# Block-wise turning through DRAM for the last layer's first six tiles, and other gather chunks

## Chip, cores and metric

One core of one Trainium2 chip. The metric is the device time of one execution in microseconds (us), as the median of several runs. PE is TensorE, DVE is VectorE, ACT is ScalarE, POOL is GpSimd and SP is SyncE, which here only issues DMAs.

## What is computed

The reference is an attention over 4 x 576 tokens with 8 heads of 64, then a mixture of 8 experts (top 2 of 8 per token, 512 to 1024 to 512), then one dense layer of 512 to 2048 to 512 with a leaky activation. The last two parts, cut to what matters here:

```python
def _moe_ref(x, w_gate, w_noise, noise, w1, w2):       # x: 2304 x 512
    ...                                                # top2, top2_w: two experts a token and their weights
    for e in range(E):
        for k in range(2):
            mask = top2[:, k] == e
            h = np.maximum(x[mask] @ w1[e], 0.0)
            out[mask] += top2_w[mask, k, None] * (h @ w2[e])

def _moe2_ref(x, w_in, w_out, alpha):
    h = x @ w_in                                       # 2304 x 2048
    g = np.maximum(h, 0.0) + alpha * np.minimum(h, 0.0)
    return g @ w_out
```

## The kernel before

The order of the work on every engine is written out by hand: instructions stand in an engine's queue in the order in which the program issues them, and each engine works its queue strictly in that order. Every product is done in three matmuls on a high and a low part of both operands (hi x hi, lo x hi, hi x lo), so each operand is split once: ACT copies the high part, DVE or POOL subtracts it for the low part.

**Tokens** go in 18 tiles of 128. Each expert has a block of two tiles and a block of three. The expert outputs are stored by slot into the DRAM tensor `yg` (L242). The last layer takes them back in token order. For one tile T it does these steps:

- `y_load(T)`: two indirect DMAs (L901), issued by POOL, gather the two expert rows of each token from `yg` into two row buffers (`m_rows`, `m_tmp`, and `m_v` for tile 0). Called gathers below.
- `combine(T)`: ACT scales the first row by its weight (L908), DVE adds the second row times its weight (L909).
- the turn: the last layer needs the tile with its 512 features on the partitions. There are two ways in the program. One is four PE transposes (L203) into a PSUM bank. The other stores the combined tile into the DRAM tensor `xs` (L1040), loads it back with four DMAs in 32x32 blocks that are already in their turned places (`blocked`, L186), and lets DVE turn the inside of every block in one instruction (L200).
- `x_split`: after the turn, ACT copies the high part out of PSUM (L206) and DVE subtracts it for the low part (L207).

**The last layer** runs over five groups of tiles, called j = 0 to 4: tiles 0 and 1, then four times four tiles. In each there are 16 chunks f of 128 hidden features. `up_chunk` is 12 matmuls (L214) into one of three PSUM banks of the ring `ps_t`; DVE applies the leaky part with two instructions (L995, L996) into a ring of four half buffers, ACT copies the high part (L999), POOL subtracts it for the low part (L1000). `down_chunk` of the same chunk follows two chunks later (L1019): per tile it reads the high, the low and the high part of the chunk in turn. `next_x(j, f)` puts the tile steps of group j + 1 between the chunks of group j. The turns of `x_split` take the bank `ps_v` for the first tile of a group and banks of the ring `ps_t` for the other three.

**Weights** of the last layer come from DRAM on SP's queue (L166, slots 72 to 79), two raw buffers deep. ACT copies the high part (L171), and POOL, or DVE for slots 72 to 74, subtracts the low part (L177). In group j = 0 the slots 75 to 79 are split at chunks 1, 3, 5, 7 and 9. The next load of a raw buffer waits for the low part of the slot before in that buffer.

**Before the change** tiles 0 and 1 are gathered during the last expert's second block, at its up chunks 5 and 7, combined during the first tile of its down products and turned by PE during the second tile. Tiles 2 to 5 are gathered at chunks 4, 6, 8 and 10 of j = 0, combined two chunks later and turned by PE two chunks after that. Tiles 6 to 17 already go through `xs` and DVE.

Of the kernel before, what the change touches and what calls it, by code (L numbers as in the profile page):

```python
# [33 lines left out]
def emit(tc, qt, kt, v, tau, wg, wn, noise, w1, w2, w_in, w_out, alpha, out):  # L34
# [3 lines left out]
    pe, dve, act, pool, sp = nc.tensor, nc.vector, nc.scalar, nc.gpsimd, nc.sync  # L38
# [4 lines left out]
    with (  # L43
# [9 lines left out]
        xs = dp.tile([N, DM], FT, name="xs")  # L53
# [126 lines left out]
        xrows = {}  # L180

        def blocked(dst, src):

            src = src.rearrange("(j a) (c i b) -> i a c j b", j=4, c=HP, i=4)
            for i in range(4):
                sp.dma_start(dst[i * 32:i * 32 + 32].rearrange("a (c j b) -> a c j b", c=HP, j=4), src[i])  # L186
# [10 lines left out]
        def x_split(src, j, x, bank=None, is_blocked=True):  # L197
            ps = (bank or (psum_v, psum_t, psum_t, psum_t)[j])()
            if is_blocked:
                dve.transpose(ps, src)  # L200
            else:
                for c in range(HP):
                    pe.transpose(ps[:, c * 128:c * 128 + 128], src[:, c * 128:c * 128 + 128], ident)  # L203
            pv_ = ps.rearrange("p (c t) -> p c t", c=HP)
            xh = x[0][:, :, j * 128:j * 128 + 128]
            act.copy(xh, pv_)  # L206
            dve.tensor_tensor(x[1][:, :, j * 128:j * 128 + 128], pv_, f32(xh), op=OP.subtract)  # L207
# [460 lines left out]
        for b in range(1, B):  # L668
            o = 20 * b
# [68 lines left out]
        for i in range(END):  # L738
# [27 lines left out]
            if outs:  # L766
                pv(iv)
                if units[iv][2] == HP - 1 or iv < SOLO:
                    T = group_evac(iv)
# [38 lines left out]
        X = (cut(m_x, 0, [HP, 384], FR), cut(m_x, 1536, [HP, 384], FR))  # L808
# [74 lines left out]
        for n in range(W0, 72):  # L883
            t = 1 + 3 * (n - W0)
# [11 lines left out]
        yrows = {}  # L896

        def y_load(T, src):
            for k in range(2):
                r = row_tile()  # L900
                pool.indirect_dma_start(  # L901
                    out=r, out_offset=None, in_=src,
                    in_offset=bass.IndirectOffsetOnAxis(ap=posi[:, T, k:k + 1], axis=0))
                yrows[T, k] = r

        def combine(T):
            y0, y1 = yrows[T, 0], yrows[T, 1]
            act.activation(y0, y0, AF.Copy, scale=wts[:, T, 0:1])  # L908
            dve.scalar_tensor_tensor(y1, y1, wts[:, T, 1:2], y0, op0=OP.mult, op1=OP.add)  # L909

        near = yg[0:N + E * BLOCK0]
        blocks = [(0, bt), (bt, CAP // 128)]
# [19 lines left out]
        for e in range(E):  # L932
            wc = [8 * e + d for d in range(4)]
            wc2 = [8 * e + 4 + d for d in range(4)]
            for bi, (t0, t1) in enumerate(blocks):
                if (e, bi) == (0, 0):
                    continue
                n = (t1 - t0) * 128
                nxt = (e, 1) if bi == 0 else (e + 1, 0)
                last = nxt[0] == E  # L940
                u0, u1 = blocks[nxt[1]]
                for f in range(8):
                    relu(f, n, mm1(psum_1(f), n, wc, X, f * 128), HS)
                    tick()
                    if last and f in (5, 7):
                        y_load((f - 5) // 2, near)
                left, owed = list(range(u1 - u0)), []
                for t in range(t1 - t0):
                    ps = psum_s()[:, 0]
                    for f in range(0, 8, 2):  # L950
                        mm2(ps, t, n, [f, f + 1], 8, wc2, HS)
                        if f % 4 == 0 and left and (t > 0 or not last):
                            j = left.pop(0)
                            x_split(yrows[j, 1] if last else xrows.pop((nxt[0], u0 + j)), j, X, None, not last)
                            if not last:
                                owed.append(j)
                        elif f % 4 == 2:
                            if last and t == 0:
                                combine(f // 4)
                            if owed:  # L960
                                owed.pop()
                                next_row()
                            tick()
                    y_store(e, t0 + t, ps)
# [62 lines left out]
        def next_x(j, f):  # L1027

            if j + 1 == len(sizes):
                return  # L1030
            T, x = sum(sizes[:j + 1]), XS[j + 1 if j < 1 else 2 - (j + 1) % 2]
            for t in range(4):
                o = 4 + 2 * t if j == 0 else 3 * t
                if f == o:
                    y_load(T + t, yg[:, :])
                if f == o + 2:
                    combine(T + t)
                    if j > 0:
                        back = xs[(T + t) * 128:(T + t) * 128 + 128]
                        sp.dma_start(back, yrows[T + t, 1])  # L1040
                        blocked(yrows[T + t, 0], back)
                if f == o + 4:
                    x_split(yrows.pop((T + t, 0 if j else 1)), t, x, None, j > 0)

        chunks = [(j, f) for j in range(len(sizes)) for f in range(16)]
        for i in range(len(chunks) + 2):
# [127 lines left out]
```

## Time and profile before

| what | value |
|---|---|
| median of 3 runs | 1166.37 us (1166.24 to 1168.17) |
| the profiled execution, its own time | 1170.81 us |
| its span in the trace | 1169.1 us |
| PE busy | 1135.2 us, 97% of the span |
| DVE, ACT, POOL busy | 53%, 46%, 46% |
| granted PE clock, mean | 0.997 of full speed |

The span is what the trace covers; the profiled execution's own time has 1.7 us around it. The profiled execution is 4.4 us above the median of the unprofiled runs. A row of the timeline gives the start in us from the span's start, the busy time, the engine, the line, the operation with what it writes and reads, and how many instructions are merged into it; in brackets stands how long the engine had been idle before it and what ended that.

### The profile page before, as it was taken

To read this page: it belongs to the slowest core of one execution; us is meant where nothing else is said; L and a number is where in the kernel's file an instruction comes from. 1 tells how busy PE (TensorE), PEld (TensorE's weight loads), DVE (VectorE), ACT (ScalarE), POOL (GpSimd) and SP (SyncE) were. 2 spreads that over 40 slices of the span, in tenths; PEclk is the share of its full clock that TensorE was granted. 3 is DMA by queue.
4 is the path that set the end of the run, shared out by engine and by line. 5 is a ranking of instruction groups with operands and counts; after the bars stand their busy time and mean duration, and the time that the engine had idled before them with its cause. 6 is when DMAs were issued, how large, how long until landed. Compare 5 with 4: busy or idle time off the path is not lost. (4 is left out here: it accounts for less than half of the span.)

```text
span 1169.1 us, 20453 instructions
## 1 busy us (share of the span) xinstructions
PE 1135.2 (97%) x7754; PEld 977.5 (84%) x7754; DVE 622.8 (53%) x1332; ACT 532.0 (46%) x1039; POOL 532.8 (46%) x632
## 2 busy tenths in 40 slices
PE   7999989999899999999999999999999999999997
PEld 6887777877789999999989898998888888888886
DVE  7978788899644544454545453445443343342221
ACT  7977768788624544444444454433211211211111
POOL 7636534654524545455454555556332333332221
PEclk9999999999999999999999999999999999999999
DMA  7423222132357676567667565541321321320001
GB/s 219 137 86 122 92 77 74 73 119 92 136 141 207 184 199 194 183 171 213 192 189 202 186 188 190 166 151 54 86 66 25 92 66 27 90 64 10 36 1 39
DMA packets 156552, 141.50 MB, mean 121 GB/s; under 512 B 108576, under 2 KB 109216, under 8 KB 156448
## 3 DMA queue, kind: packets, MB, share of 16 engines
q1 hardware_dynamic: 150400, 120.91, 35.1%
q0 software_dynamic: 5760, 18.88, 4.8%
q8 instruction: 63, 1.03, 0.4%
q14 instruction: 41, 0.34, 0.1%
q10 hardware_dynamic: 288, 0.34, 0.1%
HBM read 97.11 MB, written 42.99 MB: 120 GB/s over the span
## 5 line engine op out<-in xcount | busy, mean ns | idle before, releaser
L214 PE MATMUL ps_t<-m_v,m_pair 128*128 128x384 f32 (+2 forms) x1216 | 220.0, 317 | 0.3 <-DVE m_v L207 0.3
L177 POOL TENSOR_TENSOR m_pair<-m_v,m_pair 128x512 fp32r<-128x512 f32 x114 | 151.9, 1353 | 130.0 <-ACT m_pair L171 106.7
L214 PEld LDWEIGHTS ps_t<-m_v,m_pair 128*128 128x128 f32 x1216 | 186.8, 190 | 8.1 <-DVE m_v L207 0.5
L232 PE MATMUL ps_s<-m_pair,m_hh 128*128 128x512 f32 x528 | 167.5, 390 | 0.0
L995 DVE TENSOR_SCALAR m_tmp<-ps_t,alpha_t 128x512 f32<-128x512 f32 (+1 forms) x80 | 55.7, 697 | 208.6 <-PE ps_t L214 200.9
L225 DVE SCALAR_TENSOR_TENSOR m_gate<-ps_t,m_hh 128x384 fp32r<-128x384 f32 (+1 forms) x120 | 58.8, 493 | 169.9 <-ACT m_hh L224 169.8
L399 DVE SCALAR_TENSOR_TENSOR m_hh<-m_tmp,sm,m_hh 128x576 f32<-128x576 f32 x144 | 126.1, 908 | 2.4 <-ACT sm L380 2.0
L214 PE MATMUL ps_t<-m_v,m_early 128*128 128x256 f32 (+2 forms) x672 | 127.3, 320 | 0.0
L232 PEld LDWEIGHTS ps_s<-m_pair,m_hh 128*128 128x128 f32 x528 | 99.1, 188 | 20.3
L1000 POOL TENSOR_TENSOR m_v<-m_tmp,m_v 128x512 fp32r<-128x512 f32 x39 | 50.4, 1293 | 139.7 <-ACT m_v L999 139.7
L375 DVE TENSOR_SCALAR_CACHE_REDUCE m_tmp<-ps_s 128x576 f32<-128x576 f32 x144 | 103.6, 752 | 18.5 <-PE ps_s L364 16.0
L386 ACT ACTIVATE m_hh<-m_tmp,sm 128x576 f32<-128x576 f32 x144 | 105.7, 783 | 11.0 <-DVE m_tmp L375 10.9
L214 PEld LDWEIGHTS ps_t<-m_v,m_early 128*128 128x128 f32 x672 | 105.9, 189 | 5.1 <-DVE m_v L207 0.4
L364 PE MATMUL ps_s<-m_pair 64*128 64x288 f32 (+1 forms) x864 | 95.3, 318 | 12.9 <-DVE m_tmp L375 8.3
L999 ACT CAST m_v<-m_tmp 128x512 fp32r<-128x512 f32 x39 | 24.2, 620 | 173.5 <-DVE m_tmp L996 173.5
L232 PE MATMUL ps_s<-m_pair,m_gate 128*128 128x512 f32 x264 | 102.9, 390 | 0.0
L224 ACT ACTIVATE m_hh<-ps_t 128x384 fp32r<-128x384 f32 (+1 forms) x120 | 52.7, 439 | 98.3 <-PE ps_t L214 96.8
L1000 POOL TENSOR_TENSOR m_gate<-m_tmp,m_gate 128x512 fp32r<-128x512 f32 (+1 forms) x41 | 44.1, 1077 | 116.1 <-ACT m_gate L999 109.9
L364 PEld LDWEIGHTS ps_s<-m_pair 64*128 64x128 f32 (+1 forms) x864 | 72.3, 191 | 28.1 <-DVE m_tmp L375 14.3
L1019 PE MATMUL ps_s<-m_pair,m_v 128*128 128x512 f32 x396 | 95.1, 389 | 0.0
L1019 PE MATMUL ps_s<-m_pair,m_gate 128*128 128x512 f32 x360 | 88.3, 391 | 0.0
L1019 PEld LDWEIGHTS ps_s<-m_pair,m_v 128*128 128x128 f32 x396 | 74.3, 188 | 15.4
(229 smaller groups left out, 1982.0 us busy)
## 6 DMA issues: line engine op xcount, KB each, us to landing
m_v<-in_w_dram SPq DMA_DIRECT2D x64, 512.0 KB
yg<-m_tmp SPq DMA_DIRECT2D x40, 256.0 KB
m_tmp<-in_w_in_dram SPq DMA_DIRECT2D x16, 512.0 KB
m_tmp<-in_w_out_dram SPq DMA_DIRECT2D x16, 512.0 KB
m_early<-in_kt_dram SPq DMA_DIRECT2D x15, 320.0 KB
yg<-m_gate SPq DMA_DIRECT2D x18, 256.0 KB
m_rows<-xg SPq DMA_DIRECT2D x72, 64.0 KB
out_dram<-m_tmp SPq DMA_DIRECT2D x18, 256.0 KB
```

The lines of the kernel that those rows point to most:

```text
L177: eng.tensor_tensor(WL[n][:, w], raw[:, w], f32(WH[n][:, w]), op=OP.subtract)
L214: pe.matmul(ps[:, :n], w[wc[d]][:, col:col + 128], x[xx][:, d, :n], start=(k == 0), stop=(k == 11))
L224: act.activation(h, ps, AF.Relu)
L225: dve.scalar_tensor_tensor(hs[1][:, f * n:f * n + n], ps, 0.0, f32(h), op0=OP.max, op1=OP.subtract)
L232: pe.matmul(ps, a[:, o:o + 128], ww[w][:, c:c + 512], start=(f == 0 and k == 0), stop=(f == nf - 1 and k == 2))
L364: pe.matmul(u["ps", h][:, x, :288], lhs, kk[r, o:o + 288], start=(k == 0), stop=(k == 2))
L375: dve.tensor_scalar(u["sp"][:, h].rearrange("p (a b) -> p a b", a=2), ps[:, :, :288], -0.125, None, op0=OP.mult, op1=OP.min, accum_out=u[" ...
L386: act.activation(u["em"][:, h], u["sp"][:, h], AF.Exp, bias=u["sm"][:, h:h + 1], scale=-1.0)
L399: dve.scalar_tensor_tensor(u["em"][:, h], u["sp"][:, h], sm[:, 2 + h:3 + h], u["em"][:, h], op0=OP.is_le, op1=OP.mult, accum_out=acc)
L995: dve.tensor_scalar(g, ps, 0.0, alpha_t[:, f:f + 1], op0=OP.min, op1=OP.mult)
L1000: pool.tensor_tensor(h[:, n:2 * n], g, f32(h[:, :n]), op=OP.subtract)
L1019: pe.matmul(ps, h[x][:, t * 128:t * 128 + 128], ww[w][:, c:c + 512], start=(f == 0 and k == 0), stop=(f == 15 and k == 2))
```

## The change

Tiles 0 to 5 now take the second way, like tiles 6 to 17: `combine` itself stores every tile to `xs`, and a new function `reload` brings it back in blocks. `x_split` is called in its form for blocks everywhere, so no PE transpose is left in the last layer. In the last expert's second block, tiles 0 and 1 are gathered at up chunks 1 and 3, combined at 4 and 6 and reloaded at 6 and 7. In j = 0, tiles 2 to 5 are gathered at chunks 1, 3, 6 and 9, combined two chunks later, reloaded one chunk after that and turned five chunks after their gathers. In the later groups the gather, the combine and the turn stand where they stood.

```diff
             dve.scalar_tensor_tensor(y1, y1, wts[:, T, 1:2], y0, op0=OP.mult, op1=OP.add)
+            sp.dma_start(xs[T * 128:T * 128 + 128], y1)
+
+        def reload(T):
+            blocked(yrows[T, 0], xs[T * 128:T * 128 + 128])
...
-                    if last and f in (5, 7):
-                        y_load((f - 5) // 2, near)
+                    if last:
+                        if f in (1, 3):
+                            y_load(f // 2, near)
+                        if f in (4, 6):
+                            combine(f // 2 - 2)
+                        if f in (6, 7):
+                            reload(f - 6)
...
-                            x_split(yrows[j, 1] if last else xrows.pop((nxt[0], u0 + j)), j, X, None, not last)
+                            x_split(yrows.pop((j, 0)) if last else xrows.pop((nxt[0], u0 + j)), j, X)
...
-                            if last and t == 0:
-                                combine(f // 4)
...
-                o = 4 + 2 * t if j == 0 else 3 * t
+                o, wait = (3 * t, 4) if j else ((1, 3, 6, 9)[t], 5)
                 if f == o:
                     y_load(T + t, yg[:, :])
                 if f == o + 2:
                     combine(T + t)
-                    if j > 0:
-                        back = xs[(T + t) * 128:(T + t) * 128 + 128]
-                        sp.dma_start(back, yrows[T + t, 1])
-                        blocked(yrows[T + t, 0], back)
-                if f == o + 4:
-                    x_split(yrows.pop((T + t, 0 if j else 1)), t, x, None, j > 0)
+                if f == o + wait - 2:
+                    reload(T + t)
+                if f == o + wait:
+                    x_split(yrows.pop((T + t, 0)), t, x)
```

POOL's queue at the start of the last layer, before (L1000 is a chunk's low part, L177 a weight's low part in two halves, L901 a gather), from the low parts of chunks 0 and 1 on:

```order
L1000 TENSOR_TENSOR m_gate<-m_tmp,m_gate 128x256 x2
L177 TENSOR_TENSOR m_pair<-m_v_73,m_pair 128x512 x2
L1000 TENSOR_TENSOR m_gate<-m_tmp,m_gate 128x256 x2
L177 TENSOR_TENSOR m_pair<-m_v_73,m_pair 128x512 x2
L1000 TENSOR_TENSOR m_gate<-m_tmp,m_gate 128x256
L901 DMA m_rows<-yg,posi 128x512 x2
L1000 TENSOR_TENSOR m_gate<-m_tmp,m_gate 128x256
L177 TENSOR_TENSOR m_pair<-m_v_73,m_pair 128x512 x2
L1000 TENSOR_TENSOR m_gate<-m_tmp,m_gate 128x256
L901 DMA m_tmp<-yg,posi 128x512 x2
```

The same stretch of POOL's queue after the change (L1007 is the former L1000):

```order
L1007 TENSOR_TENSOR m_gate<-m_tmp,m_gate 128x256 x2
L177 TENSOR_TENSOR m_pair<-m_v_73,m_pair 128x512 x2
L901 DMA m_rows<-yg,posi 128x512 x2
L1007 TENSOR_TENSOR m_gate<-m_tmp,m_gate 128x256 x2
L177 TENSOR_TENSOR m_pair<-m_v_73,m_pair 128x512 x2
L901 DMA m_tmp<-yg,posi 128x512 x2
L1007 TENSOR_TENSOR m_gate<-m_tmp,m_gate 128x256 x2
L177 TENSOR_TENSOR m_pair<-m_v_73,m_pair 128x512 x2
L1007 TENSOR_TENSOR m_gate<-m_tmp,m_gate 128x256
L901 DMA m_rows<-yg,posi 128x512 x2
```

The gathers of tiles 2 and 3 now stand directly behind the low parts of weights 75 and 76 and ahead of the low parts of chunks 2 and 4.

DVE's queue in the same group after the change, from the combine of tile 2 (L909) to the turn of tile 3 (L1002 and L1003 are the former L995 and L996, chunks 4 to 8):

```order
L909 SCALAR_TENSOR_TENSOR m_rows<-m_rows,wts 128x512
L1002 TENSOR_SCALAR m_tmp<-ps_t,alpha_t 128x256
L1003 SCALAR_TENSOR_TENSOR m_tmp<-ps_t,m_tmp 128x256
L1002 TENSOR_SCALAR m_tmp<-ps_t,alpha_t 128x256
L1003 SCALAR_TENSOR_TENSOR m_tmp<-ps_t,m_tmp 128x256
L909 SCALAR_TENSOR_TENSOR m_tmp<-m_tmp,wts 128x512
L1002 TENSOR_SCALAR m_tmp<-ps_t,alpha_t 128x256
L1003 SCALAR_TENSOR_TENSOR m_tmp<-ps_t,m_tmp 128x256
L200 STREAM_TRANSPOSE ps_v<-m_rows 128x512
L207 TENSOR_TENSOR m_hh<-ps_v,m_hh 128x4x128
```

Before, the first combine stood three chunks later and there was no turn on DVE; now both stand between the leaky steps of the chunks.

SP's queue there after the change, from the load of weights 77 and 78 on (L910 is the store to `xs`):

```order
L166 DMA m_v_73<-wf_out 128x2x512 x2
L910 DMA xs<-m_rows 128x512
L186 DMA m_rows<-xs 32x16x32 x4
L166 DMA m_v_73<-wf_out 128x2x512
L910 DMA xs<-m_tmp 128x512
L186 DMA m_tmp<-xs 32x16x32 x4
```

Before, the three weight loads stood in a row with nothing between them; now the store and reload of tile 2 stand ahead of the third load, and the store of tile 3 behind it.

## Rows read from the trace of the kernel before

**Rows 1.** The page, busy time of each engine with its share of the span.

```profile
PE 1135.2 (97%) x7754; PEld 977.5 (84%) x7754; DVE 622.8 (53%) x1332; ACT 532.0 (46%) x1039; POOL 532.8 (46%) x632
```

**Rows 2.** Table, group j = 0: us, busy by engine, clock, DMA share, GB/s.

```profile
767.00:811.00 44.00, 44.00 (x294) 40.38 (x293) 22.63 (x40) 16.06 (x29) 31.88 (x33) 1.00 0.32 100
```

**Rows 3.** Timeline of PE, turns of tiles 0 and 2, chunks beside them, first of j = 1.

```profile
756.25 0.39 PE L232 MATMUL ps_s<-m_pair,m_hh 128*128 128x512 f32 x1
...
756.98 0.48 PE L232 MATMUL ps_s<-m_pair,m_hh 128*128 128x512 f32 x1
...
777.03 1.55 PE L1019 MATMUL ps_s<-m_pair,m_gate 128*128 128x512 f32 x6
...
784.06 1.24 PE L214 MATMUL ps_t<-m_v,m_early 128*128 128x256 f32 x9
...
786.88 1.60 PE L214 MATMUL ps_t<-m_v,m_pair 128*128 128x256 f32 x12
788.31 0.60 PE L203 MATMUL ps_v<-ident,m_rows 128*128 128x128 f32 x4
788.67 1.64 PE L1019 MATMUL ps_s<-m_pair,m_gate 128*128 128x512 f32 x6
790.15 1.60 PE L214 MATMUL ps_t<-m_v,m_pair 128*128 128x256 f32 x12
...
811.21 2.20 PE L214 MATMUL ps_t<-m_hh,m_early 128*128 128x512 f32 x9
```

**Rows 4.** Timeline of POOL, start of j = 0.

```profile
772.57 2.54 POOL L177 TENSOR_TENSOR m_pair<-m_v,m_pair 128x512 fp32r<-128x512 f32 x2 [0.21 <-ACT m_pair L171]
775.06 1.55 POOL L1000 TENSOR_TENSOR m_gate<-m_tmp,m_gate 128x256 fp32r<-128x256 f32 x2
...
780.21 0.97 POOL L901 DMA_INDIRECT m_rows<-yg,posi  x1
781.48 0.95 POOL L901 DMA_INDIRECT m_rows<-yg,posi  x1 [0.30 <-issue]
782.45 0.74 POOL L1000 TENSOR_TENSOR m_gate<-m_tmp,m_gate 128x256 fp32r<-128x256 f32 x1
```

**Rows 5.** Timeline of DVE, j = 0 and a turn in j = 1.

```profile
783.46 0.42 DVE L996 SCALAR_TENSOR_TENSOR m_tmp<-ps_t,m_tmp 128x256 f32<-128x256 f32 x1
785.25 1.69 DVE L909 SCALAR_TENSOR_TENSOR m_rows<-m_rows,wts 128x512 f32<-128x512 f32 x1 [1.36 <-DMA m_rows<-yg,posi]
...
804.86 0.75 DVE L909 SCALAR_TENSOR_TENSOR m_tmp<-m_tmp,wts 128x512 f32<-128x512 f32 x1 [1.30 <-DMA m_tmp<-yg,posi]
...
850.96 0.72 DVE L200 STREAM_TRANSPOSE ps_t<-m_tmp 128x512 f32<-128x512 f32 x1
852.33 0.69 DVE L207 TENSOR_TENSOR m_gate<-ps_t,m_v 128x512 fp32r<-128x512 f32 x1 [0.65 <-ACT m_v L206]
```

**Rows 6.** Timelines of POOL and ACT, first gather of tile 0, second of tile 5.

```profile
748.62 1.01 POOL L901 DMA_INDIRECT m_v<-yg,posi  x1 [0.16 <-issue]
...
753.92 0.72 ACT L908 ACTIVATE m_v<-m_v,wts 128x512 f32<-128x512 f32 x1 [2.67 <-DMA m_v<-yg,posi]
...
801.28 0.95 POOL L901 DMA_INDIRECT m_tmp<-yg,posi  x1 [0.30 <-PE ps_t L203]
```

**Rows 7.** Timeline of SP: loads of weights 73 and 74; store and reload of tile 7.

```profile
755.98 2.06 SPq L166 DMA_DIRECT2D m_v<-wf_out  x2
...
842.84 0.33 SPq L1040 DMA_DIRECT2D xs<-m_tmp  x1
844.86 2.59 SPq L186 DMA_DIRECT2D m_tmp<-xs  x4
```

**Rows 8.** Table by stage, behind that reload.

```profile
849.00:849.50 0.50, 0.50 (x4) 0.41 (x3) 0.00 (x0) 0.00 (x0) 0.38 (x1) 1.00 0.05 8
```

**Rows 9.** Table by stage, a fall of the granted clock in the attention.

```profile
118.00:121.00 3.00, 1.75 (x14) 1.10 (x14) 2.52 (x6) 1.70 (x3) 2.31 (x8) 1.00 0.44 150
121.00:125.00 4.00, 4.00 (x40) 3.01 (x39) 3.84 (x12) 1.37 (x5) 2.25 (x3) 0.57 0.77 281
```

## The prediction

> **What bounds the kernel now.** I read the busy line first: PE works 97% of the span [rows 1]. Then I read the table by stage for the part that the change touches. In group j = 0 of the last layer PE is busy for the whole 44 us at full clock, while POOL is busy for 31.9 us of the same 44 [rows 2]. So PE's row of instructions sets the time there, every microsecond taken off PE is a microsecond gained, and every wait of PE is one lost. POOL has 12 us to spare, but it works a queue in order, and what counts is when each low part comes out of it. The timelines of POOL, DVE and SP then say how far each of them is ahead of PE [rows 4, 5, 7].
>
> **What the change takes off PE.** Six turns go. In j = 0 a chunk with a turn takes 3.27 us from up to up (786.88 to 790.15), one without 2.82 (784.06 to 786.88), so a turn costs 0.45 us [rows 3]; four of them are 1.80. Of the 0.45 the transposes themselves hold 0.36 (788.31 to 788.67), and the step behind them is longer by 0.09. A plain step is (1.48 - 0.09) / 6 = 0.23 us (six from 788.67 to 790.15). For tile 0 the matmul behind the turn starts 0.73 us after the one ahead of it (756.25 to 756.98) [rows 3], so that turn costs 0.50 + 0.09 = 0.59. Tile 1 is taken at 0.45. Together 1.80 + 0.59 + 0.45 = 2.84 us. If nothing came late, the time would be 1166.37 - 2.84 = 1163.5.
>
> The Trainium skill, VectorE: DVE Perf Modes, section The three transpose paths, lists 390 ns for one 128x128 turn on TensorE and 311 ns on VectorE (for bf16), and its rules for authors say to turn on TensorE when PSUM is the target, which speaks against this change. As an estimate from that page, 24 transposes would free 24 x 0.39 = 9.4 us instead of 2.84; the trace does not agree, since four transposes hold PE for 0.36 us [rows 3], and the sum stays with the rows.
>
> **What it adds on POOL.** I lay out j = 0 in the new order, instruction by instruction, with the durations of the rows and PE starting where it does now; done with the old order, the same layout starts j = 1 at 811.2, where the trace has it [rows 3], and PE waits nowhere. A weight's low part takes 2.54 us, a chunk's low part 0.74, and a pair of gathers 2.24 (780.21 to 782.45) [rows 4] with 0.16 ahead of it [rows 6], 2.4 in all. Before, the low parts of chunks 2 and 3 follow weight 75 at once (775.06) [rows 4]. Now tile 2's gathers stand between: they run from 775.1 to 777.5, and chunk 2's low part ends at 778.25. PE starts down chunk 2 at 777.03 with a matmul on the high part and needs the low part 0.23 later [rows 3]. **PE waits 1.05 us.** Then the low part of chunk 3, that of weight 76 (to 781.5), tile 3's gathers (to 783.9), and chunk 4's low part ends at 784.65, where PE, now 1.05 late, wants it at 783.94: **0.75 us.** These two need nothing but POOL's order and durations.
>
> **What it adds on DVE.** DVE works in order too, and now has two kinds of waits in its queue, with the leaky steps of the next chunks queued behind them, and behind those ACT's copies, POOL's low parts and PE's banks. First the combines: the add starts 3.7 us after its second gather starts (781.48 to 785.25, waiting for the DMA) and takes 1.7 while POOL works, 0.75 while POOL rests [rows 4, 5]. Tile 2's second gather starts at 776.5, so DVE adds from 780.2 to 781.9. Tile 3's starts at 782.9, so DVE stands until 786.6 and adds until 788.3; only then come the steps of chunk 6, which before were done at 783.9 [rows 5]. Its low part ends at 790.5 and PE waits another 0.25. Second the turns: a turn takes 0.70, then DVE stands 0.65 for ACT's copy and subtracts in 0.69 [rows 5], 2.04 us in all. The turn must wait for the reload. Store to first reload issue is 2.02 us, the four issues take 2.6 [rows 7], and the DMA engines fall quiet just behind 849.0 (a share of 0.05 in the next half microsecond) [rows 8], 1.6 us after the last issue; I take 2.0 until DVE may start. The upper bound is 3.5, for DVE starts that tile's turn at 850.96 straight behind its own work [rows 5].
>
> For tile 2 that is just in time (store 782.0, reload landed 788.6, DVE free 789.3). **Tile 3 is the bad one.** Its add ends at 788.3; its store stands on SP behind the load of weight 79, which waits for weight 77's low part (787.9), so that does not delay it further; reload issued from 790.4, landed 795.0. DVE comes to the turn at 793.2 and stands until 795.0. Behind it are tile 4's add and chunk 9's leaky steps, done at 798.8. ACT's copies of chunk 9 and of weight 79 follow (to 800.2), POOL does chunk 9's low part, weight 79's low part to 802.8, tile 5's gathers to 805.2, and chunk 10's low part to 805.95. PE wants that at 802.9: **3.08 us, the largest wait.** On the way PE waits 0.59 for the bank of chunk 7, 0.28 at chunk 8 and 0.20 at chunk 9.
>
> At the end, tile 5: second gather 804.2, add 807.9 to 808.7, reload landed 815.35, turn, copy, subtraction to 817.4. PE could start j = 1 at 815.6: **1.85 us.** Waits in all: 1.05 + 0.75 + 0.25 + 0.59 + 0.28 + 0.20 + 3.08 + 1.85 = 8.05. Less 1.80 for four turns, j = 0 ends 6.2 us later.
>
> **Bounds.** With a gather at 3.58 us (801.28 to 804.86) [rows 5, 6] and a reload at 1.6, the same layout gives +5.3. With the slowest gather, 5.3 us (748.62 to 753.92, beside a weight load and a store) [rows 6] it gives +9.6. With the reload at its bound 3.5 it gives +9.4. Tile 3's gathers and tile 2's reload are in flight together with weight 78, so I give each 0.5 us more: **+7.2 for j = 0.**
>
> **The last expert's block.** Tiles 0 and 1 free 1.04 us of PE. Their gathers, from 748.62 before [rows 6], move ahead by four up chunks, to behind the store of the expert's first block; I put their start at 740. Laid out in the same way, the reloads are issued from about 753 to 758, ahead of the load of weight 73 on SP, which before went out at 756 [rows 7]. ACT's copy and DVE's low part of weight 73 stand ahead of tile 1's copy and turn, so the second tile is ready at about 766.4, and PE, 1 us early, wants it at 766.0: a wait of 0.4, from 0 if that start is 1 us earlier to 1.5 if it is 1 us later. Net -0.6. The later groups keep their order and shift as a whole, cost nothing.
>
> **Sum.** +7.2 - 0.6 = +6.6 us. Against the profiled execution that is 1170.81 + 6.6 = 1177.4; against the median 1166.37 + 6.6 = **1173.0**. A measurement of this kernel tells about 0.2% (2.3 us) from no change.
>
> **Rivals.**
>
> All hidden: the turns fall off PE and everything else fits. That is 1163.5, faster. It decides at chunk 2's low part, which has to end by 777.26; with the gathers ahead of it there are 2.15 us from 775.1 for a pair of gathers and 0.74 of low part, so the pair would have to hold POOL for under 1.4 us. For it speaks that POOL is idle 28% of j = 0 [rows 2]; against it that the pair holds POOL for 2.24 us in the rows [rows 4].
>
> Only POOL's two waits: the gathers and reloads land early enough that DVE never stands in front of a leaky step that PE needs. Then 1163.5 + 1.05 + 0.75 = 1165.3, no change. It asks that tile 3's reload lands 1.8 us earlier than in the layout and its gathers about 2 us earlier. Against it: even before, at the same two chunks' distance, DVE stood 1.36 and 1.30 us for gathers that POOL had issued on time [rows 5].
>
> The clock falls as well: PE stands for 3 us at chunk 10 and again before j = 1. In the attention PE was busy only 1.75 of 3 us, and the granted clock then was 0.57 on average over the next 4 us [rows 9], between full speed, 2.4 GHz, and half, 1.2. That is 4 x 0.43 = 1.7 us of work lost. So 1173.0 + 1.7 = 1174.7. Against it: I found only this one fall in the attention, which has many gaps of PE. The Trainium skill, TensorE: Matmul & The Clock Gate, Part 1, says that an idle stretch puts the array back to half clock; the trace shows that, once.
>
> **How the numbers follow.** Forecast (waits as laid out, full clock) 0.63, clock falls too 0.19, only POOL's waits 0.12, all hidden 0.06. Range: the low end is the layout with quick DMAs, 5.3 - 1.0 = +4.3 or 1170.7, lowered to 1169 for half of chunk 10's wait staying away; the high end is slow gathers, a late first block and the clock, 9.6 - 1.04 + 1.5 + 1.7 = +11.8 or 1178. Below it lie the last two rivals, about 0.18. Chances: faster 0.06, same 0.13, slower 0.81.
>
> **What would show it.** On PE in j = 0: no L203, and waits released by POOL's low part at down chunks 2 and 4 of about 1 us each, a wait of about 3 us at chunk 10, and one of about 2 us on DVE's L207 before j = 1. On DVE: idle time in front of L909 and L200 that ended by a DMA. On POOL: gathers from 775 on. It is wrong if PE stays busy through j = 0, or if the reloads land under 1 us after their issue.

## The result, and the profile after

The changed kernel takes 1183.58 us (median of 5 runs, 1182.76 to 1184.69) against 1167.64 for the kernel before in the same comparison. The ratio is 1.0136 (1.0121 to 1.0151), so it is 15.9 us slower; the forecast was 1173.0 with 1169 to 1178. One of the five executions of the kernel before took 2233.24 us; without it its median is 1167.0, and the difference 16.6 us. The profiled execution's own time is 1183.75, with a span of 1182.0.

The two profiled executions differ elsewhere too (the one of before lost some 3.5 us more in the attention), so I compare the stretch that the change touches, from the first matmul of the last expert's second block to the first up matmul of j = 1. Timeline of PE: the start of the stretch, of the kernel before and then of the changed kernel; its end before is in [rows 3], the one after stands further down.

```profile
732.97 16.83 PE L214 MATMUL ps_t<-m_v,m_pair 128*128 128x384 f32 x96
...
729.42 16.83 PE L214 MATMUL ps_t<-m_v,m_pair 128*128 128x384 f32 x96
```

Before, the stretch is 811.21 - 732.97 = 78.24 us, now 824.30 - 729.42 = 94.88: **+16.6 us**. From there to the end both kernels take the same within 0.2 us. Of the 16.6, +2.85 lie in the expert's block (to up chunk 0) and +13.8 in j = 0.

The page after, busy time of the engines; it answers to [rows 1].

```profile
PE 1140.5 (96%) x7730; PEld 980.2 (83%) x7730; DVE 622.5 (53%) x1338; ACT 532.4 (45%) x1039; POOL 532.1 (45%) x632
```

The 24 transposes are gone (x7730 against x7754), and yet PE is busy for 5.3 us more. What that is stands in PE's timeline of the changed kernel: the rows with waits, and up chunks 0, 9 and 13 beside one at full speed (the one at 800.80). In brackets, idle time and what ended it; L214 is up, L1026 down, L1007 POOL's low part.

```profile
766.38 2.80 PE L214 MATMUL ps_t<-m_v,m_early 128*128 128x256 f32 x9 [3.78 <-ACT m_v L206]
...
780.56 1.45 PE L1026 MATMUL ps_s<-m_pair,m_gate 128*128 128x512 f32 x5 [0.81 <-POOL m_gate L1007]
...
787.13 1.43 PE L1026 MATMUL ps_s<-m_pair,m_gate 128*128 128x512 f32 x5 [0.65 <-POOL m_gate L1007]
...
796.42 2.93 PE L214 MATMUL ps_t<-m_v,m_pair 128*128 128x256 f32 x12 [1.93 <-DVE m_tmp L1003]
...
800.80 1.60 PE L214 MATMUL ps_t<-m_v,m_pair 128*128 128x256 f32 x12
...
812.64 1.90 PE L1026 MATMUL ps_s<-m_pair,m_gate 128*128 128x512 f32 x5 [2.78 <-POOL m_gate L1007]
814.35 2.68 PE L214 MATMUL ps_t<-m_v,m_pair 128*128 128x256 f32 x12
...
824.30 0.50 PE L214 MATMUL ps_t<-m_hh,m_early 128*128 128x512 f32 x1 [0.25 <-ACT m_hh L206]
```

Two things are to be seen. There are waits, where [rows 2] had none: 3.78 us ahead of up chunk 0, then at down chunks 2 and 4, up chunk 9 and down chunk 10. And behind three of them the same matmuls take nearly twice as long (12 in 2.93 or 2.68 us against 1.60). The table by stage says why: behind the length of the stretch stand busy time by engine, the granted PE clock, DMA share and GB/s.

```profile
765.50:772.50 7.00, 5.97 (x26) 5.68 (x27) 3.11 (x6) 2.91 (x5) 0.73 (x1) 0.51 0.65 199
796.00:800.00 4.00, 3.58 (x15) 3.45 (x16) 1.18 (x3) 1.66 (x3) 3.49 (x4) 0.57 0.73 176
813.00:817.00 4.00, 4.00 (x18) 3.67 (x17) 2.16 (x4) 1.13 (x2) 0.53 (x2) 0.57 0.29 112
773.00:795.00 22.00, 20.00 (x122) 17.00 (x120) 7.71 (x15) 7.32 (x12) 16.51 (x17) 1.00 0.48 139
```

The clock fell to half, from 2.4 to 1.2 GHz, three times. Busy time times what the clock lacks, in half microseconds, is 2.95 + 1.63 + 1.71 = 6.3 us of lost work. So the 16.6 us are: turns -2.7 (0.93, what is left of the expert's block beside its wait, and the 1.80 of the forecast), the wait ahead of up chunk 0 +3.8, waits in j = 0 +9.3 (13.8 + 1.8 - 6.3, counted from chunk to chunk, so with the small gaps that the rows don't show), clock +6.3. The 1.80 is not measured by itself; it fits that a chunk of j = 0 without a wait now takes 2.80 us (818.26 to 821.06), as one without a turn did before.

What the engines behind those waits stand for is in the other timelines of the changed kernel. SP first: L166 is a weight load, L910 the store of a tile, L186 its reload; the first fence is the expert's block, the second j = 0.

```profile
749.64 0.37 SPq L166 DMA_DIRECT2D m_v<-wf_out  x1
750.06 0.46 SPq L878 DMA_DIRECT2D wf_out<-m_tmp  x1
750.61 0.38 SPq L910 DMA_DIRECT2D xs<-m_rows  x1
751.09 2.91 SPq L186 DMA_DIRECT2D m_v<-xs  x4
755.22 2.60 SPq L186 DMA_DIRECT2D m_rows<-xs  x4
757.92 1.07 SPq L166 DMA_DIRECT2D m_v<-wf_out  x2
```

```profile
783.70 0.36 SPq L166 DMA_DIRECT2D m_v<-wf_out  x1
784.26 0.33 SPq L910 DMA_DIRECT2D xs<-m_rows  x1
788.60 3.13 SPq L186 DMA_DIRECT2D m_rows<-xs  x4
791.90 0.51 SPq L166 DMA_DIRECT2D m_v<-wf_out  x1
792.45 0.47 SPq L910 DMA_DIRECT2D xs<-m_tmp  x1
797.01 2.60 SPq L186 DMA_DIRECT2D m_tmp<-xs  x4
804.57 0.34 SPq L910 DMA_DIRECT2D xs<-m_rows  x1
806.61 2.82 SPq L186 DMA_DIRECT2D m_rows<-xs  x4
```

From a store to its first reload it is 4.34 us for tile 2 (784.26 to 788.60) and 4.56 for tile 3 (792.45 to 797.01), but 2.04 for tile 4, as in [rows 7]. The two slow ones have a weight load issued just ahead of them, the quick one has none. For tile 1 it is 4.61 (750.61 to 755.22), but there SP issues the reload of tile 0 in between, until 754.00, and stands still only for the last 1.2 us; a weight load and another store are ahead of it.

POOL of the changed kernel, the first gather of tile 0, which waited for the store of the expert's first block:

```profile
737.80 1.01 POOL L901 DMA_INDIRECT m_v<-yg,posi  x1 [4.87 <-DMA yg<-m_tmp]
```

ACT of the changed kernel, copies of weight 73 (L171) and of tile 1 (L206); the row ahead of them is the copy of weight 73 in the kernel before.

```profile
759.46 1.05 ACT L171 CAST m_pair<-m_v 128x1024 fp32r<-128x1024 f32 x1 [1.61 <-DMA m_v<-wf_out]
...
762.77 1.04 ACT L171 CAST m_pair<-m_v 128x1024 fp32r<-128x1024 f32 x1 [4.99 <-DMA m_v<-wf_out]
765.75 0.58 ACT L206 CAST m_v<-ps_t 128x512 fp32r<-128x512 f32 x1 [1.93 <-DVE ps_t L200]
```

Weight 73 landed 3.48 us after its issue before (755.98 in [rows 7] to 759.46), and 4.85 now (757.92 to 762.77), behind the reloads of two tiles and with the next load issued right behind it. Tile 1's turn on DVE stands behind weight 73's low part, so its copy comes at 765.75, while PE was free at 762.6.

DVE of the changed kernel in j = 0, combine of tile 3, turns of tiles 2 and 3; they answer to [rows 5].

```profile
789.96 0.84 DVE L909 SCALAR_TENSOR_TENSOR m_tmp<-m_tmp,wts 128x512 f32<-128x512 f32 x1 [4.01 <-ACT m_tmp L908]
...
793.45 0.73 DVE L200 STREAM_TRANSPOSE ps_v<-m_rows 128x512 f32<-128x512 f32 x1 [1.78 <-DMA m_rows<-xs]
...
801.79 0.73 DVE L200 STREAM_TRANSPOSE ps_t<-m_tmp 128x512 f32<-128x512 f32 x1 [4.58 <-DMA m_tmp<-xs]
```

### The profile page after: what moved, and what is told of

The parts are those of the page before. It is cut to its first block, busy times and chain, and to the rows that moved or that the text cites. A ratio compares the mean times of both kernels' runs of the same rounds, so it can differ in the third digit from the quotient of the medians.

```text
span 1182.0 us, 20477 instructions
## 1 busy us (share of the span) xinstructions
PE 1140.5 (96%) x7730; PEld 980.2 (83%) x7730; DVE 622.5 (53%) x1338; ACT 532.4 (45%) x1039; POOL 532.1 (45%) x632
## 5 line engine op out<-in xcount | busy, mean ns | idle before, releaser
L214 PE MATMUL ps_t<-m_v,m_pair 128*128 128x384 f32 (+2 forms) x1216 | 223.3, 321 | 2.3 <-DVE m_tmp L1003 1.9
L177 POOL TENSOR_TENSOR m_pair<-m_v,m_pair 128x512 fp32r<-128x512 f32 x114 | 151.8, 1352 | 128.6 <-ACT m_pair L171 98.5
L214 PEld LDWEIGHTS ps_t<-m_v,m_pair 128*128 128x128 f32 x1216 | 189.7, 193 | 11.2 <-DVE m_tmp L1003 2.4
L1002 DVE TENSOR_SCALAR m_tmp<-ps_t,alpha_t 128x512 f32<-128x512 f32 (+1 forms) x80 | 55.7, 696 | 201.5 <-PE ps_t L214 201.5
L214 PE MATMUL ps_t<-m_v,m_early 128*128 128x256 f32 (+2 forms) x672 | 129.7, 324 | 3.9 <-ACT m_v L206 3.8
L214 PEld LDWEIGHTS ps_t<-m_v,m_early 128*128 128x128 f32 x672 | 107.8, 193 | 9.7 <-ACT m_v L206 4.2
L1007 POOL TENSOR_TENSOR m_v<-m_tmp,m_v 128x512 fp32r<-128x512 f32 x39 | 50.4, 1292 | 139.3 <-ACT m_v L1006 139.3
L1007 POOL TENSOR_TENSOR m_gate<-m_tmp,m_gate 128x512 fp32r<-128x512 f32 (+1 forms) x41 | 44.0, 1077 | 131.7 <-ACT m_gate L1006 125.7
L1026 PE MATMUL ps_s<-m_pair,m_v 128*128 128x512 f32 x396 | 95.1, 389 | 0.0
L1026 PE MATMUL ps_s<-m_pair,m_gate 128*128 128x512 f32 x360 | 90.2, 394 | 4.9 <-POOL m_gate L1007 4.5
L1026 PEld LDWEIGHTS ps_s<-m_pair,m_v 128*128 128x128 f32 x396 | 74.4, 188 | 15.4
```

The source lines that it names most:

```text
L177: eng.tensor_tensor(WL[n][:, w], raw[:, w], f32(WH[n][:, w]), op=OP.subtract)
L214: pe.matmul(ps[:, :n], w[wc[d]][:, col:col + 128], x[xx][:, d, :n], start=(k == 0), stop=(k == 11))
L1002: dve.tensor_scalar(g, ps, 0.0, alpha_t[:, f:f + 1], op0=OP.min, op1=OP.mult)
L1007: pool.tensor_tensor(h[:, n:2 * n], g, f32(h[:, :n]), op=OP.subtract)
L1026: pe.matmul(ps, h[x][:, t * 128:t * 128 + 128], ww[w][:, c:c + 512], start=(f == 0 and k == 0), stop=(f == 15 and k == 2))
```

## Experiments

**Theories.** The forecast's own theory, the layout, has three parts: POOL's order makes two waits, DVE standing for gathers and reloads makes the rest, and the clock stays up. Its rivals after the result: that the first block is what went wrong, not j = 0; that the clock's falls are the missing part, or that they only show and cost nothing; that another placing of the gathers would have mended j = 0. For every run I give the ratio with its interval to the kernel before in the same comparison, the times as medians, and the stretch against 78.24 us. The stretch is that of one profiled execution, the time a median of several, so the two can differ by a microsecond or two. The kernel before took 1167.21 us beside the first four runs, 1171.72 beside the next four, 1169.22 beside the last two.

**One half each.** Tiles 0 and 1 alone the new way (diffs are against the changed kernel):

```diff
-                o, wait = (3 * t, 4) if j else ((1, 3, 6, 9)[t], 5)
+                o = 4 + 2 * t if j == 0 else 3 * t
...
-                    x_split(yrows.pop((T + t, 0)), t, x)
+                    x_split(yrows.pop((T + t, 0 if j else 1)), t, x, None, j > 0)
```

> Only tiles 0 and 1 take the new way; tiles 2 to 5 are gathered and turned by PE as before. Theory (late weight 73 plus clock): PE waits 3.8 us for tile 1's split before the first up chunk, the granted clock falls to half behind that and costs 3.0 us, and two turns are gone (-0.9): +5.9 us against the kernel before, about 1.005. Rival (the clock fall is a bystander, because PE would wait anyway): +2.9 us, 1.0025. Rival (the early gathers cost nothing, all loss lies in j = 0): -0.9 us, 0.999.

Measured 1.0057 (1.0037 to 1.0076), 1173.06 us, the stretch +4.7. The wait ahead of up chunk 0 is there as in the full change, 3.68 us, and behind it the clock loses 1.6 us of work.

Tiles 2 to 5 alone:

```diff
-                        if f in (1, 3):
-                            y_load(f // 2, near)
...
+                    if last and f in (5, 7):
+                        y_load((f - 5) // 2, near)
...
-                            x_split(yrows.pop((j, 0)) if last else xrows.pop((nxt[0], u0 + j)), j, X)
+                            x_split(yrows[j, 1] if last else xrows.pop((nxt[0], u0 + j)), j, X, None, not last)
```

> Only tiles 2 to 5 take the new way with gathers at chunks 1, 3, 6 and 9; tiles 0 and 1 are turned by PE as before. Theory: the waits of j = 0 as in the changed kernel, 9.2 us, less four turns (-1.8), plus two clock falls behind the waits of 1.9 and 2.8 us (+3.4): +10.8 us, about 1.0093. Rival (clock is a bystander): +7.4 us, 1.006. Rival (the loss of j = 0 is a consequence of its late and slow start): near 0.

Measured 1.0089 (1.0071 to 1.0107), 1177.96 us, the stretch +12.1, of which 3.1 us are lost to the clock, here behind down chunk 10 alone. The halves add up: 4.7 + 12.1 = 16.8 against 16.6. So the first block is a little under a third of the loss, and each half misses its forecast (-0.6 and +7.2) by about 5 us.

**The first block's wait.** The reload of tile 1 goes behind the load of weight 73:

```diff
+        put2(191, lambda: reload(1))
         for n in range(72, 75):
...
-                        if f in (6, 7):
-                            reload(f - 6)
+                        if f == 6:
+                            reload(0)
```

> The changed kernel with one step moved on SP's queue: tile 1's reload is issued behind the load of weight 73 instead of ahead of it. Theory: weight 73 is split about 4 us earlier, tile 1 is ready near the point where PE wants it, the wait of 3.8 us before the first up chunk shrinks to under 0.5 us and the clock fall of 3.0 us behind it goes: -6.5 us against the changed kernel, 1.008 of the kernel before. Rival (tile 1 is late because of its own gather, store and reload): the wait stays, no gain.

Measured 1.0086 (1.0069 to 1.0103), 1177.52 us, 6.1 us less than the full change, the stretch +10.1. ACT gets weight 73 at 758.51 in this run, and PE doesn't wait at up chunk 0:

```profile
758.51 1.05 ACT L171 CAST m_pair<-m_v 128x1024 fp32r<-128x1024 f32 x1 [0.46 <-DMA m_v<-wf_out]
```

With it the first fall of the clock is gone too. The order on SP is the cause of this wait: tile 1's reload comes as late behind its store as before (750.96 to 755.46), and that costs nothing here.

**Does the clock cost anything by itself?** The changed kernel with PE kept at work through the first wait:

```diff
+        ps = psum_v()
+        for i in range(14):
+            pe.matmul(ps, hh[:, 0:128], WH[60][:, 0:512], start=True, stop=True)
```

> The changed kernel with 14 extra matmuls of 512 columns (3.1 us at full clock, result unused) in front of the first up chunk, in the place where PE stands idle for 3.8 us. They add work and take nothing away. Theory (the idle stretch makes the clock fall, and the slow matmuls behind it cost 3.0 us): the wait becomes work, the clock stays full, and the time falls by about 3 us against the changed kernel, to 1.011 of the kernel before. Rival (the slow stretch is hidden behind POOL and DVE): no change, 1.0136. Rival (extra matmuls just add): +3 us, 1.016.

Measured 1.0117 (1.0097 to 1.0136), 1181.30 us, 2.3 us less than the full change although PE does more; the stretch +14.6. The two intervals overlap (1.0121 to 1.0151 for the full change), so the sign of this difference is likely and its size is not certain. Table by stage, 762 to 824 (clock 0.97; it is 0.89 in the full change), and PE's timeline at up chunk 9:

```profile
762.00:824.00 62.00, 51.96 (x298) 43.48 (x297) 27.00 (x48) 19.33 (x33) 31.40 (x33) 0.97 0.45 127
```

```profile
794.64 1.69 PE L214 MATMUL ps_t<-m_v,m_pair 128*128 128x256 f32 x12 [2.70 <-DVE m_tmp L1006]
```

The lost work goes from 6.3 to 1.5 us, more than the filling aimed at: the clock did not fall at up chunk 9 either, although the wait there is longer (2.70 against 1.93). But of these 4.8 us only 2.1 to 2.3 come back, and 0.5 of the stretch's 2.1 because up chunk 0 itself started earlier (36.42 us after the start of the stretch against 36.96); j = 0 is shorter by 1.5. The shown waits of j = 0 sum to 9.9 us here (with a new one of 1.13 at up chunk 11) and to 7.3 in the full change: a PE that is quicker reaches POOL and DVE earlier and waits longer for them. So the clock's falls seem to cost something, and less than the table says.

**The first half mended.** Tiles 0 and 1 alone, with the reload of tile 1 behind weight 73, that is, the edits of the first and the third run together:

> Only tiles 0 and 1 take the new way, and tile 1's reload stands behind the load of weight 73. Tiles 2 to 5 as before. Theory: the wait before the first up chunk and the clock fall behind it are gone, two turns are saved: between -0.9 and +0.5 us against the kernel before, 0.999 to 1.0005; a difference under 2.3 us can't be told from none. Rival (the early gathers, stores and reloads cost PE time by themselves): +3 to +6 us, 1.0025 to 1.005.

Measured 0.9992 (0.9982 to 1.0003), 1170.75 us, in the expected range and not apart from no change; the stretch +0.2, so no gain is seen there. Of the 1.04 us of turns, waits of 0.43 us ahead of up chunk 0 and 0.34 in it take most.

**Other placings of tiles 2 to 5** (tiles 0 and 1 as before). Gathers at chunks 2, 4, 6 and 8, stored and reloaded two chunks later and turned six chunks after the gather, with a third pair of row buffers:

```diff
-        row_tile.aps = rows[2:] + [raw64[:, :512], raw64[:, 512:]]
+        row_tile.aps = rows[2:] + [raw64[:, :512], raw64[:, 512:]] + rows[:2]
...
-                o, wait = (3 * t, 4) if j else ((1, 3, 6, 9)[t], 5)
+                o, wait = (3 * t, 4) if j else (2 + 2 * t, 6)
...
-                if f == o + wait - 2:
+                if f == o + 2:
                     reload(T + t)
```

> Only tiles 2 to 5 take the new way, but gathered at chunks 2, 4, 6 and 8 (no weight is split there), stored and reloaded at the combine two chunks later and turned six chunks after the gather; a third pair of row buffers lets them. Theory (POOL's queue and DVE standing in front of turns that are not loaded yet): no wait over 1.2 us, waits of 1.5 to 4 us in all against 1.8 saved, so 0 to +3 us against the kernel before, up to 1.0025, and the granted clock full in j = 0 if no wait reaches 2 us. Rival (the second way itself costs DVE and DMA too much in j = 0, wherever its steps stand): near the run with only tiles 2 to 5 changed, +9 to +11 us, 1.008 to 1.009.

Measured 1.0036 (1.0022 to 1.0049), 1175.97 us: +4.2 (2.6 to 5.7), a little over the expected range, the stretch +2.6. The rows with waits of PE in j = 0, and the table over the same 62 us:

```profile
792.63 1.43 PE L1025 MATMUL ps_s<-m_pair,m_gate 128*128 128x512 f32 x5 [0.61 <-POOL m_gate L1006]
800.75 1.69 PE L214 MATMUL ps_t<-m_v,m_pair 128*128 128x256 f32 x12 [0.39 <-issue]
816.85 0.50 PE L214 MATMUL ps_t<-m_hh,m_early 128*128 128x512 f32 x1 [1.12 <-ACT m_hh L206]
```

```profile
762.00:824.00 62.00, 59.46 (x344) 50.68 (x343) 27.40 (x50) 20.50 (x35) 34.16 (x35) 1.00 0.48 132
```

With one more chunk between gather and turn, gathers away from the weights' chunks and reloads issued one chunk sooner, the waits are short and the clock stays full. The three were changed together, and no run takes them apart; the next one, with moved gathers and the distance left at five, makes the distance the likely main part. The stores of tiles 2 to 4 were as slow here (4.33, 4.76 and 4.34 us to the reload): with enough distance that costs little.

Gathers at 2, 4, 7 and 9 with the distance of five, to see whether POOL's order at chunks 1 and 3 is the root:

```diff
-                o, wait = (3 * t, 4) if j else ((1, 3, 6, 9)[t], 5)
+                o, wait = (3 * t, 4) if j else ((2, 4, 7, 9)[t], 5)
```

> Only tiles 2 to 5 take the new way; gathers at chunks 2, 4, 7 and 9, all other steps at the same distances as in the changed kernel. Theory: POOL's two waits at chunks 2 and 4 (1.0 and 0.8 us) go, but DVE still stands before the turn of tile 3, so that a wait of 3 to 4 us stays at a chunk between 8 and 10 and one of 2 to 3 before j = 1, with clock falls behind them: +6 to +9 us, 1.005 to 1.008. Rival (POOL's order at chunks 1 and 3 is the root of all later waits): near 0.

Measured 1.0074 (1.0053 to 1.0095), 1181.30 us, the stretch +9.2. POOL's two waits at down chunks 2 and 4 are gone, and one of 0.62 for POOL stands at down chunk 6; but DVE's are 2.51 and 2.20, one of 2.82 stands ahead of j = 1, and the clock loses 3.2 us, half of it behind the first matmul of j = 1. POOL's order at chunks 1 and 3 is not the root.

Tile 3 alone one chunk later (gathers at 1, 4, 6 and 9):

```diff
-                o, wait = (3 * t, 4) if j else ((1, 3, 6, 9)[t], 5)
+                o, wait = (3 * t, 4) if j else ((1, 4, 6, 9)[t], 5)
```

> Only tiles 2 to 5 take the new way; as in the changed kernel except that tile 3 is gathered at chunk 4 instead of 3. Theory (gathers in flight double the time of a store next to them): tile 2's store then has no gather beside it and its reload is issued 2.0 to 2.5 us after it instead of 4.3; POOL's wait at chunk 4 goes; in all 1 to 3 us less than the run with only tiles 2 to 5 changed, +8 to +10 us, about 1.0075. Rival (weight loads make the store slow, not gathers): 4.3 us stays.

Measured 1.0084 (1.0069 to 1.01), 1181.23 us, +9.5, the stretch +8.8. The time is as expected, its reason is not: with tile 3's gathers out of the way tile 2's store should have been quick again, and SP still stood 4.15 us. My theory, that gathers slow this store, fell with this.

**What slows the store.** Tiles 2 to 5 alone the new way, and once the loads of weights 77 to 79 left out, once tile 3's gathers replaced by fills on POOL:

```diff
             wraw[n] = raw
+            if n >= 77:
+                return
```

> Tiles 2 to 5 the new way, tiles 0 and 1 as before, and the loads of weights 77, 78 and 79 left out (their raw buffers keep the weights 75 and 76, so the last layer is computed with wrong output weights). Open is what makes SP's wait between the store of tile 2 and its first reload 4.32 us instead of the 2.02 of the kernel before: the load of weight 78, issued ahead of the store, or tile 3's gathers, running beside it. Theory: the weight load; then this stretch is 2.0 to 2.6 us here for tile 2, that of tile 3 also, the wait at chunk 9 (2.30 with the loads) falls below 0.8, and the stretch from the last expert's second block to j = 1 comes to 85 to 88 us against 90.3. Rival: the gathers; then tile 2's stretch stays above 3.8 us, the wait at chunk 9 above 1.7, and the stretch at 89 to 91.

```diff
+                if T == 3:
+                    pool.memset(r, 0.0)
+                    continue
```

> Tiles 2 to 5 the new way, tiles 0 and 1 as before, all weights loaded, and tile 3's two gathers replaced by two fills with zero on POOL (so tile 3 is wrong). Theory, the weight load makes the store slow: SP's stretch from the store of tile 2 to its first reload stays above 3.8 us. Rival, the gathers make it slow: it falls to 2.0 to 2.6 us. If either alone is enough or both share it, the stretch lies between, at 2.8 to 3.6 us, in this run and in the run without weight loads. DVE no longer stands for tile 3's gathers here, so the wait at chunk 9 falls below 1 us by every theory.

SP's timeline, without the weight loads (L913 store, L188 reload) and then without tile 3's gathers (L915, L186):

```profile
779.28 0.33 SPq L913 DMA_DIRECT2D xs<-m_rows  x1
781.33 2.61 SPq L188 DMA_DIRECT2D m_rows<-xs  x4
785.85 0.33 SPq L913 DMA_DIRECT2D xs<-m_tmp  x1
787.88 2.60 SPq L188 DMA_DIRECT2D m_tmp<-xs  x4
```

```profile
778.07 0.36 SPq L166 DMA_DIRECT2D m_v<-wf_out  x1
778.63 0.33 SPq L915 DMA_DIRECT2D xs<-m_rows  x1
782.98 2.71 SPq L186 DMA_DIRECT2D m_rows<-xs  x4
```

2.05 and 2.03 us without the loads, 4.35 with a load and no gather: for tile 2 it is the weight load just ahead on SP's queue. Without the loads the time was 1177.33 (one run, +8.1) and the stretch +8.95 against +12.1, and the wait at up chunk 9 is gone; the wait at down chunk 10 stays. Without tile 3's gathers it was 1178.53 (one run, +9.3), the stretch +10.6, and the wait at up chunk 9 did not fall below 1 us as I expected of every theory: it is 2.88. So that wait belongs to tile 2's reload, not to tile 3's gathers. PE's timeline, down chunk 10 of the run without loads, up chunk 9 of the run without the gathers:

```profile
805.00 2.50 PE L1026 MATMUL ps_s<-m_pair,m_gate 128*128 128x512 f32 x5 [2.80 <-POOL m_gate L1007]
...
790.79 1.70 PE L214 MATMUL ps_t<-m_v,m_pair 128*128 128x256 f32 x12 [2.88 <-DVE m_tmp L1005]
```

A weight load is enough to slow a store, but it is not the only thing that does. In the run with gathers at 2, 4, 7 and 9 no load is near the store of tile 4, and it still took 3.99 us to the reload, with tile 5's two gathers issued 1.7 and 0.4 us ahead of it. SP's timeline, then POOL's:

```profile
804.17 0.34 SPq L911 DMA_DIRECT2D xs<-m_rows  x1
808.16 2.60 SPq L186 DMA_DIRECT2D m_rows<-xs  x4
```

```profile
802.51 0.97 POOL L901 DMA_INDIRECT m_tmp<-yg,posi  x1
803.78 1.18 POOL L901 DMA_INDIRECT m_tmp<-yg,posi  x1 [0.30 <-issue]
```

In the same run tile 5's store, issued right behind tile 4's reload with no load near, took 4.68. Whether it is the place in the queue or the traffic as such that makes a store slow, no run separates.

## Why the prediction was right or wrong, step by step

**The miss in one sum.** The stretch missed its +6.6 by 10.0 us: 6.3 of the clock, which the forecast put at nothing, 3.4 of the wait ahead of up chunk 0, and 0.3 in j = 0, where the waits come to 9.3 against the 9.0 laid out (8.05 + 1.0). That the waits of j = 0 agree in sum is in part luck: those behind the slow stores were longer and the one ahead of j = 1 was shorter.

**What bounds the kernel, and the turns: right.** Every wait of PE stands in the time. The turns gave back 0.93 of their 1.04 us in the expert's block; the 1.80 of j = 0 fits the rows and is not measured by itself.

**POOL's two waits: right.** Forecast 1.05 and 0.75; counted from where the low part is needed (0.23 us behind the chunk's first matmul) they are 0.97 and 0.81. In the run without tile 3's gathers the second one is gone, and with gathers at 2, 4, 7 and 9 both are.

**DVE's waits: the place at chunk 10 right, the durations wrong.** Down chunk 10 was forecast at 3.08 us and is 2.78 to 2.80 (2.94 to 2.96 counted as for POOL's waits) in the full change, in its second half alone and without weight loads. PE's timeline, up chunk 11, of the changed kernel and then of the run without weight loads:

```profile
803.91 1.69 PE L214 MATMUL ps_t<-m_v,m_pair 128*128 128x256 f32 x12
...
796.27 1.70 PE L216 MATMUL ps_t<-m_v,m_pair 128*128 128x256 f32 x12 [0.47 <-DVE m_hh L209]
```

From there to the end of the wait at down chunk 10 it is 8.73 us in both (803.91 to 812.64, 796.27 to 805.00). Tile 3's turn lets PE go on at up chunk 11, and the same turn starts the row of work on DVE, ACT and POOL that down chunk 10 waits for: so where PE stands for the turn at up chunk 11, this wait has one length however late the turn comes, and a quicker transfer does not shorten it. The wrong step is "Store to first reload issue is 2.02 us", read from a store with no load ahead of it [rows 7] and set in where two of four stand right behind a weight load: there it is 4.3 to 4.6. "For tile 2 that is just in time" fell with it: DVE stood 1.78 us for that reload, and up chunk 9 waited 1.93. I named the load of weight 79 in front of tile 3's store, but only asked when SP could issue the store, not how long it would then take. The gathers were slower than my 3.7 us too (tile 3's first, issued at 783.84, was scaled by ACT at 789.20), but the run without them shows that this did not set the wait at chunk 9. For shared traffic I allowed 1.0 us; the runs with and without loads differ by 3.1. Without the loads, and less the clock's 3.0, j = 0 is +5.9 us, where the layout without that allowance gave +6.2; that is one execution, and its waits do not agree one by one (there is none ahead of j = 1). Nor did the reload keep to its 2.0 us, at most 3.5: without the loads tile 3's turn came 3.66 us behind the last issue (790.48 to 794.14), with tile 4's gathers in flight beside it.

**The wait ahead of j = 1: smaller.** Forecast 1.85; the rows show 0.25 and another 0.22. PE came there later, held up by the half clock; that this is why, no run shows.

**The last expert's block: wrong.** The forecast was a wait of 0.4, at most 1.5; it was 3.78. The step saw the right order (two reloads ahead of weight 73 on SP, weight 73 ahead of tile 1 on ACT and DVE) and mis-sized what stands ahead of that load. Counted from the block's first matmul, the load of weight 73 went out at 28.5 us (757.92 - 729.42), where the layout has 25.0 (758 - 732.97). Of these 3.5 us, 1.35 are the first gather, put at 740 and started 8.38 us into the block, where 740 means 7.03; 1.2 are SP standing for tile 1's store, which has no term in the layout's 753 to 758; 0.9 I can't assign. The load then landed 4.85 us after its issue instead of 3.48. Moving one reload took the wait away.

**The clock: a rival with 0.19 that came true three times over.** I priced one fall at 1.7 us and asked for waits of 3 us; the lost work was 6.3. The argument against it, one fall only in an attention full of gaps, weighed too much. The fill suggests that a third to a half of the lost work is real time (1.5 in j = 0 to 2.3 in the median, of 4.8) and the rest only takes the place of waits. By halves: the first block missed by 5.3 us, 3.3 of wait and 1.6 of clock; j = 0, alone, by 4.9, of which the clock is 3.1 and longer waits 1.8.

**The range.** Its high end put one slow gather, a first block late by 1.5 and one fall of the clock together; it had no term for a store slowed by what was issued just ahead of it, and priced one fall of the clock where three came.

## What to carry to other kernels

A transfer's duration is to be read from a row with the same neighbours, on its own queue and on the others: one with nothing ahead of it says little of one that stands behind a large load. Where work is taken off a full engine and its data then takes a longer way, lay the way out with such rows and give it the distance first, one chunk more than the sum needs; here one chunk more, with evenly spaced gathers and sooner reloads, took the stretch from +12.1 to +2.6 us, for a prize of 1.8. And a wait of PE can have a second price, the clock behind it: here falls stood behind waits of 1.93 us and more, though not behind all of them, so a layout that shows such waits is to carry a term for it.

## What the runs showed of the hardware

A 256 KB store to DRAM lets its reload start after 2.0 us when nothing was issued just ahead of it, and after 4.15 to 5.01 (13 stores in seven runs) behind a 512 KB load issued 0.5 to 0.7 us before. Right behind a reload it was anything from 2.54 to 4.68 (five stores). With gathers on POOL's queue it was both: 2.05 where one was issued 0.4 us ahead and one behind, 3.99 where both were issued ahead. The Trainium skill, DMA: Bandwidth & Descriptors, section Two DMAs through the same engine are not ordered, says that descriptors of one queue start in order and then overlap. A store that is slow behind a load on its own queue fits that; the store that was slow beside another queue's gathers is not explained by it.

The length of a PE wait does not say whether the clock falls behind it. Waits of 1.93, 2.78 and 3.78 us were followed by half clock, those of 2.30 (tiles 2 to 5 alone), 2.70 (the filled run) and 2.88 (the run without tile 3's gathers) by 12 matmuls at full speed. The Trainium skill, TensorE: Matmul & The Clock Gate, Part 1, names an idle stretch as what puts the clock down; that is so here, but no row tells beforehand which one will. What in a stretch decides stays open.
